# Decode attention: three 64 KiB places that hold K and then V, in place of four 32 KiB buffers and a weight buffer

## The chip, the cores and the metric

The kernel runs on one core of a Trainium2 chip. The metric is device time in microseconds (us), one execution at a time, given as the median and the range of several executions.

Engines: PE is the matrix engine (PEld its weight loads), DVE the vector engine, ACT the scalar engine, SP the engine that issues DMA transfers. "Landing" is the arrival of a transfer.

## The reference, cut to what matters

One token, 16 heads, 65536 cached keys a head, 256 numbers a key, all bf16. K and V together are 1.07 GB, and every byte is used once.

```python
# x [1,1,448]; k_cache, v_cache [1,16,65536,256]; wq [448,4096]; wo [4096,448]
# w1 [448,1792]; w2 [1792,448]
xn = layernorm(x)
q  = (xn @ wq).reshape(1, 1, 16, 256).transpose(0, 2, 1, 3)
p  = softmax(einsum("bhqd,bhkd->bhqk", q, k_cache) * 256 ** -0.5)
s  = einsum("bhqk,bhkd->bhqd", p, v_cache)      # then heads joined, @ wo
g  = silu(silu(xn @ w1) @ w2)
return x + s * g
```

## The kernel before

The keys of a head are cut into four blocks of 128 x 128 keys, so there are 64 blocks. Of each block a partition holds 128 keys. K and V come in half blocks: a row of 64 keys x 256 x 2 bytes is 32 KiB a partition, 4 MiB in all. Four such buffers, two for K and two for V, hold them, and a fifth, W, holds weights.

DVE works through a half block in two steps of 32 keys. In each step it multiplies the last 13 keys with the query in one wide product, which ACT then sums key by key, and does the other 19 as fused dot products. PE weighs V with the softmax weights. Each block keeps its own maximum; the blocks of a head are joined at the end.

```python
KT, SUB, ND, TPB = 64, 32, 19, 2
Kt = [pool.tile([P, KT * Dh], bf16, name=f"K{t}") for t in range(TPB)]
Vt = [pool.tile([P, KT * Dh], bf16, name=f"V{t}") for t in range(TPB)]
W = pool.tile([P, max(DF * HD + HD // 2, NHA * D, KT * Dh)], bf16, name="W")
prod = [pool.tile([P, NA, Dh], bf16, name=f"prod{i}") for i in range(2)]
# ... (small tiles cut)

def sp_block(i):
    for t in range(TPB):
        take(sp, kf[t])                       # K buffer free?
        sp.dma_start(out=Kt[t][:, :], in_=src(Kd, i, t)).then_inc(kl[t], 16)
        take(sp, vf[t])
        sp.dma_start(out=Vt[t][:, :], in_=src(Vd, i - 1, t)).then_inc(vl[t], 16)

def dve_block(i, first=False, halves=False):
    # ... (query copy, waits cut)
    for t in range(TPB):
        for s in range(2):
            m = dve.tensor_tensor(out=prod[k % 2][:, :, :], ...)   # 13 keys, for ACT
            m.then_inc(mr, 1)
            for j in range(ND):                                    # 19 keys
                ins = dve.tensor_tensor_reduce(out=junk_d[jk][:, :], ...)
    # ... copy of the scores, maximum

with nc.Fori(1, NBLK - 1, 1, engines={ET.PE, ET.DVE, ET.Activation, ET.SP}, ...) as i:
    sp_block(i)
    dve_block(i)
    act_block(i)
    # ... PE: maximum, V of the block before, turn of the output
```

## Time and profile before

| | before |
|---|---|
| time, median of 4 (range) | 2529.26 us (2528.97 to 2529.54) |
| span of the profiled execution | 2527.2 us |
| HBM read | 1084.29 MB |
| DMA, mean over the span | 429 GB/s |
| K or V transfers of 4 MiB | 251 |
| packets of 32 KiB / median duration of one | 32128 / 1218 ns |
| last input landed | 2519.7 us |

The prediction below shows the main views: a DMA row of nines, so the time is reading. Two more lines of the page of the kernel before, the busy times and the packet count, will be set against those of the kernel after:

```profile
PE 1284.5 (51%) x4945; PEld 483.4 (19%) x4945; DVE 2219.2 (88%) x10276; ACT 1446.6 (57%) x6996; POOL 1.4 (0%) x12
...
DMA packets 40450, 1084.46 MB, mean 429 GB/s; under 512 B 4338, under 2 KB 6516, under 8 KB 6644
```

The first gives, for each engine, busy microseconds, share of the span and number of instructions. DVE at 88% is the engine nearest to becoming a bound; everything else has room.

### The profile page before, as it was taken

What the parts mean: (1) busy time and instruction counts of PE and PEld (TensorE: products, weight loads), DVE (VectorE), ACT (ScalarE), POOL (GpSimd) and SP (SyncE); (2) the same over time, 40 slices, a digit from 0 to 9 for tenths busy, and PEclk for the clock granted to TensorE, in tenths of its full rate; (3) what the DMA queues carried; (4) which work ended last, traced back from release to release, by engine and by line L of the source; (5) the groups of instructions that cost most, each with busy time, mean ns of one, the idle gap of its engine ahead of it and who ended that gap; (6) DMA issues with size and microseconds to landing.
All of it is one profiled execution on the core that took longest, in us unless ns stands there. A gap on an engine that the chain in (4) does not pass through costs nothing. (4 is left out here: it accounts for less than half of the span.)

```text
span 2527.2 us, 30558 instructions
## 1 busy us (share of the span) xinstructions
PE 1284.5 (51%) x4945; PEld 483.4 (19%) x4945; DVE 2219.2 (88%) x10276; ACT 1446.6 (57%) x6996; POOL 1.4 (0%) x12
## 2 busy tenths in 40 slices
PE   3554455455544554555455445544554455445547
PEld 1111121111111211111112111111121111111212
DVE  7989898898898988988989889889898898898886
ACT  5656565655565656555656565556565655565553
POOL 0000000000000000000000000000000000000000
PEclk7777777777777777777767776777677767776778
DMA  9999999999999999999999999999999999999998
GB/s 413 432 432 432 432 432 432 432 432 432 432 432 433 432 433 432 432 432 432 432 432 432 432 432 432 432 432 432 432 432 432 432 432 433 432 432 432 432 432 346
DMA packets 40450, 1084.46 MB, mean 429 GB/s; under 512 B 4338, under 2 KB 6516, under 8 KB 6644
## 3 DMA queue, kind: packets, MB, share of 16 engines
q1 hardware_dynamic: 40434, 1084.31, 99.8%
q8 instruction: 4, 0.07, 0.0%
q14 instruction: 10, 0.08, 0.0%
q10 hardware_dynamic: 2, 0.00, 0.0%
HBM read 1084.29 MB, written 0.00 MB: 429 GB/s over the span
## 5 line engine op out<-in xcount | busy, mean ns | idle before, releaser
L262 ACT ACTIVATE junk_a<-prod 128x256 bf16<-128x256 bf16 x3328 | 1330.7, 401 | 746.9 <-ACTq L141 746.9
L308 PE MATMUL psO<-V,PV 128*2 128x512 bf16 x4064 | 1165.2, 458 | 1097.6 <-PEq L141 1097.6
L226 DVE CUSTOM_DVE_ANT_0 junk_d<-K,qcur 128x256 bf16<-128x256 bf16 x4864 | 1698.7, 414 | 0.0
L308 PEld LDWEIGHTS psO<-V,PV 128*2 128x2 bf16 x4064 | 388.4, 97 | 1847.6 <-issue 1520.3
L212 DVE TENSOR_TENSOR prod<-K,qcur 128x3328 bf16<-128x3328 bf16 x256 | 482.9, 1886 | 247.0 <-DVEq L141 247.0
L262 ACT ACTIVATION_READ_ACCUMULATOR junk_a<-prod 128x1 f32 x3328 | 620.0, 186 | 0.0
L226 DVE DVE_READ_ACCUMULATOR2_ANT S<- 128x1 f32 x4864 | 374.2, 77 | 0.0
L295 ACT COPY O<-psO 2x512 f32<-2x512 f32 x64 | 36.8, 574 | 202.4 <-ACTq L141 202.4
L343 PE MATMUL ps_t<-eye,O 2*128 2x1 f32 x520 | 69.6, 251 | 48.4 <-PEq L141 48.4
L343 PEld LDWEIGHTS ps_t<-eye,O 2*128 2x128 f32 x520 | 65.9, 192 | 69.0 <-issue 68.9
L297 ACT COPY hist<-ps_t 128x2 f32 (+1 forms) x65 | 10.4, 160 | 94.9 <-ACTq L141 94.9
L301 PE MATMUL ps_nb<-gmax,ones_row 1*128 1x1 bf16 x65 | 10.3, 159 | 56.1 <-PEq L141 55.6
L191 DVE COPY qcur<-qb 128x256 bf16 (+1 forms) x64 | 14.5, 227 | 25.4 <-issue 15.8
L284 ACT ACTIVATE PV<-S,hist 128x128 bf16<-128x128 f32 (+1 forms) x65 | 26.0, 400 | 2.1
L199 DVE COPY S<-S 128x128 f32<-128x128 f32 (+1 forms) x65 | 14.7, 226 | 9.5
L200 DVE TENSOR_REDUCE rmax<-S 128x1 bf16<-128x128 f32 (+1 forms) x65 | 18.2, 280 | 0.2 <-issue 0.2
L180 DVE TENSOR_REDUCE gmax<-ps_m 1x1 bf16<-1x128 f32 x65 | 17.8, 274 | 0.5 <-DVEq L141 0.5
L301 PEld LDWEIGHTS ps_nb<-gmax,ones_row 1*128 1x128 bf16 x65 | 6.0, 92 | 60.8 <-issue 60.5
L333 PE MATMUL ps_m<-ident,rmax 128*1 128x128 bf16 x65 | 14.3, 220 | 5.7 <-PEq L141 5.7
L488 PE MATMUL ps_a<-xnT,V 128*64 128x1 bf16 x112 | 6.7, 256 | 18.2 <-DMA V<-in_B_w_dram 18.2
L284 ACT ACTIVATION_READ_ACCUMULATOR PV<-S,hist (+1 forms) x65 | 12.1, 186 | 0.0
L488 PEld LDWEIGHTS ps_a<-xnT,V 128*64 128x64 bf16 x112 | 6.6, 210 | 18.7 <-DMA V<-in_B_w_dram 18.7
(65 smaller groups left out, 79.3 us busy)
## 6 DMA issues: line engine op xcount, KB each, us to landing
K<-in_A_k_cache_dram SPq DMA_DIRECT2D x126, 4096.0 KB, 21.3
V<-in_A_v_cache_dram SPq DMA_DIRECT2D x125, 4096.0 KB, 28.7
K<-in_A_k_cache_dram SPq DMA_DIRECT2D x4, 2048.0 KB, 18.5
V<-in_A_v_cache_dram SPq DMA_DIRECT2D x4, 2048.0 KB, 22.9
W<-in_A_v_cache_dram SPq DMA_DIRECT2D x2, 2048.0 KB, 27.3
W<-in_A_wq_dram SPq DMA_DIRECT2D x1, 3072.0 KB, 10.4
K<-in_A_wo_dram SPq DMA_DIRECT2D x3, 896.0 KB, 31.4
V<-in_B_w_dram SPq DMA_DIRECT2D x1, 1568.0 KB, 35.5
```

Source lines behind the costliest of these rows:

```text
L180: dve.reduce_max(out=gmax[0:1, :], in_=ps_m[0:1, :], axis=AX.X).then_inc(gm, 1)
L191: q_t = own(dve.tensor_copy(out=qcur[:, :], in_=qb[:, sub(q0, Dh)]))
L199: dve.tensor_copy(out=S2[:, c0:c1], in_=S[:, c0:c1]).then_inc(f, 1)
L200: dve.reduce_max(out=rmax[:, :], in_=S[:, c0:c1], axis=AX.X).then_inc(rm, 1)
L212: m = dve.tensor_tensor(out=prod[k % 2][:, :, :], in0=Kv[:, s * SUB + ND : (s + 1) * SUB, :], in1=qcur[:, None, :].to_broadcast([P, NA, Dh ...
L226: ins = dve.tensor_tensor_reduce(out=junk_d[jk][:, :], in0=Kv[:, s * SUB + j, :], in1=qcur[:, :], scale=1.0, scalar=0.0, op0=ALU.mult, op1 ...
L262: ins = act.activation(out=junk_a[jk][:, :], in_=prod[k % 2][:, j, :], func=ACT.Identity, accum_out=S[:, a : a + 1],)
L284: act.activation(out=PV[:, c0:c1], in_=S2[:, c0:c1], func=ACT.Exp, bias=neg, scale=scale, accum_out=hist[:, at(i), 1:2].rearrange("p o s - ...
L295: act.copy(out=O[:, :], in_=po[:, :]).then_inc(oc, 1)
L301: pe.matmul(ps_nb[:, 0:1], lhsT=ones_row[0:1, :], rhs=gmax[0:1, :], start=True, stop=True).then_inc(bm, 1)
L308: ins = pe.matmul(po[:, :], lhsT=PV[:, c0 + c : c0 + c + 2], rhs=T[:, (k0 + c) * Dh : (k0 + c + 2) * Dh], start=(start and c == 0), stop=( ...
L343: ins = pe.matmul(ps_t[:, a : a + 1], lhsT=Ov[:, j, a, :], rhs=eye2[:, j : j + 1], start=(j == 0), stop=(j == 1),)
```

## The change

The intent is to move the same bytes in half as many, twice as long transfers. A block's K takes one 64 KiB row a partition, in one of three places. When DVE and ACT have done with it, V of the same block is loaded into the same place, one block late; when PE has done with V, K of the block three later follows. To make room, the products and the unused outputs are written over K itself, and all weights lie in a place that is not used yet (at the start) or no longer (at the end). DVE, ACT, PE and SP each get a loop of their own, three blocks long, because there are three places. At the start w1 comes before wq, and the first K comes in two halves. The diff, cut to its core:

```diff
-KT = 64
+KB = 128
 SUB = 32
 ND = 19
-TPB = 2
+NR = 3
...
-    Kt = [pool.tile([P, KT * Dh], bf16, name=f"K{t}") for t in range(TPB)]
-    Vt = [pool.tile([P, KT * Dh], bf16, name=f"V{t}") for t in range(TPB)]
-    W = pool.tile([P, max(DF * HD + HD // 2, NHA * D, KT * Dh)], bf16, name="W")
-    prod = [pool.tile([P, NA, Dh], bf16, name=f"prod{i}") for i in range(2)]
+    KW, HK = KB * Dh, KB // 2
+    R = [pool.tile([P, KW], bf16, name=f"R{t}") for t in range(NR)]
...
+    def load_k(i, s):
+        take(sp, vf[s])
+        sp.dma_start(out=R[s][:, :], in_=block(Kd, i)).then_inc(kl[s], 16)
+        sp.sem_inc(kh[s], 16)
+
+    def load_v(i, s):
+        take(sp, kf[s])
+        sp.dma_start(out=R[s][:, :], in_=block(Vd, i)).then_inc(vl[s], 16)
...
+            m = dve.tensor_tensor(out=pair, in0=pair, ...)       # in place
...
+                ins = dve.tensor_tensor_reduce(out=Kv[:, c, :], in0=Kv[:, c, :], ...)
...
+        load_rows(w1_t, B_w1, F, dl["w1"])
+        load_rows(wq_t, A_wq, HD, dl["wq"])
+        load_keys(R[0], block(Kd, 0), 0, HK, kl[0])
+        # ... w2
+        load_keys(R[0], block(Kd, 0), HK, KB, kh[0])
+        load_k(1, 1)
+        load_k(2, 2)
+        load_v(0, 0)
+        load_v(1, 1)
+        with loop(ET.SP, NR, LAST - 2, NR) as i:
+            for s in range(NR):
+                load_k(i + s, s)
+                load_v(i + s - 1, (s - 1) % NR)
...
+        with loop(ET.DVE, 0, LAST - 2, NR, hint_back_edge=True) as i:
+            for s in range(NR):
+                dve_block(s)
...
+        with loop(ET.PE, 1, LAST - 4, NR, hint_back_edge=True) as i:
+            for s in range(NR):
+                pe_block(i + s, s)
```

The last block is peeled off the loops, with V in pieces (the last 128 keys as 32, 32, 32, 16, 8, 8) and the projection `wo` behind it.

## The prediction

> **What bounds the kernel now.** I read the page first, then the waits of the DMA-issuing queue, then one iteration in the timeline, then the chain that ended last. The page, top and DMA rows:
>
> ```profile
> span 2527.2 us, 30558 instructions
> ...
> DMA  9999999999999999999999999999999999999998
> GB/s 413 432 432 432 432 432 432 432 432 432 432 432 433 432 433 432 432 432 432 432 432 432 432 432 432 432 432 432 432 432 432 432 432 433 432 432 432 432 432 346
> ...
> HBM read 1084.29 MB, written 0.00 MB: 429 GB/s over the span
> ```
>
> All 16 DMA engines are busy from the first slice to the last but one, at 432 GB/s. 1084.29 MB / 432 GB/s is 2510 us of the 2527. The kernel is bound by its reads; only some 17 us are not the steady stream. The issues show that each transfer is queued well ahead:
>
> ```profile
> K<-in_A_k_cache_dram SPq DMA_DIRECT2D x126, 4096.0 KB, 21.3
> V<-in_A_v_cache_dram SPq DMA_DIRECT2D x125, 4096.0 KB, 28.7
> ...
> SPq L141 <- SPq L141: 2316.3, 251, 24.3
> ```
>
> 4 MiB moves in 4.19 MB / 432 GB/s = 9.7 us, yet takes 21 to 29 us from issue to landing, so 12 to 19 us of that is queue ahead of it. The last line, from the waits of the issuing queue, says that SP itself waits nearly all the time for a buffer to come free; that costs nothing while the queue is so deep. This depth is what the change spends. Next the work that frees buffers:
>
> ```profile
> L262 ACT ACTIVATE junk_a<-prod 128x256 bf16<-128x256 bf16 x3328 | 1330.7, 401 | 746.9 <-ACTq L141 746.9
> L308 PE MATMUL psO<-V,PV 128*2 128x512 bf16 x4064 | 1165.2, 458 | 1097.6 <-PEq L141 1097.6
> L226 DVE CUSTOM_DVE_ANT_0 junk_d<-K,qcur 128x256 bf16<-128x256 bf16 x4864 | 1698.7, 414 | 0.0
> ```
>
> and one buffer (half a block) in the timeline near 1000 us:
>
> ```profile
> 1003.84 1.89 DVE L212 TENSOR_TENSOR prod<-K,qcur 128x3328 bf16<-128x3328 bf16 x1 [2.52 <-DVEq L141]
> 1012.22 1.89 DVE L212 TENSOR_TENSOR prod<-K,qcur 128x3328 bf16<-128x3328 bf16 x1
> 1013.45 9.00 PE L308 MATMUL psO<-V,PV 128*2 128x512 bf16 x32 [10.95 <-PEq L141]
> 1020.82 0.23 DVE L199 COPY S<-S 128x128 f32<-128x128 f32 x1
> 1021.29 0.33 SPq L174 DMA_DIRECT2D K<-in_A_k_cache_dram  x1
> ```
>
> The reader is to see: one DVE step (one product, 19 dot products) is 1012.22 - 1003.84 = 8.38 us; from the start of DVE on a landed buffer to the issue that reuses it is 1021.29 - 1003.84 = 17.45 us for two steps, hence 17.45 + 2 x 8.38 = 34.2 us for four. The K landing before it had its last of 16 engines done at 1003.13 in the packet records, 0.7 us ahead of DVE. Last, the end, from the timeline:
>
> ```profile
> 2512.39 3.62 PE L308 MATMUL ps_a<-W,PV 128*2 128x512 bf16 x16
> 2515.84 1.68 PE L679 MATMUL ps_ao<-K,OT 128*1 128x448 bf16 x8
> 2518.48 4.70 PE L679 MATMUL ps_ao<-K,OT 128*1 128x448 bf16 x24
> ...
> 2523.22 0.61 DVE L688 TENSOR_TENSOR tmp<-ps_ao,g_f 1x448 f32<-1x448 f32 x1 [3.71 <-PE ps_ao L679]
> 2523.86 0.61 DVE L692 TENSOR_TENSOR out_bf<-tmp,x_f 1x448 bf16<-1x448 f32 x1
> 2524.50 0.33 SPq L696 DMA_DIRECT2D out_dram<-out_bf  x1
> ```
>
> In the packet records the first data packet starts at 2.0 us and the last input lands at 2516.0 us. So 11.2 us of the span come after the data: PE is behind by then.
>
> [...]Here the first issue starts at 0.96 and the first packet at 2.0 us, so I use 1.1. [...]in the burst at 1013.45 the first ten weight loads are 0.43 us apart, later ones 0.21. [...]The trace has such packets, of 8 and 16 KB, but none between 83 and 2467 us[...]. Each one seen stretches the data packet behind it: the two at 57.4 and 82.7 us cost one and the same DMA engine 333 ns plus 657 ns each.
>
> **The change, part by part.**
> *Buffers.* K of a block (8 MiB, 8.39 / 0.432 = 19.4 us) goes into a place; when DVE is done, its V goes into the same place; when PE is done, the K of three blocks later. Order in the queue: K(i+1), V(i), K(i+2), V(i+1). A pair takes 38.8 us. V(i) may start when K(i+1) is in, 19.4 + 19.4 = 38.8 us after K(i) landed. It is ready to start 0.7 (wake) + 34.2 (DVE) + 1.1 (first packet) = 36.0 us after. Slack 2.8 us. K(i+2) may start 58.2 us after K(i) landed. Before it: DVE done at 34.7, maximum through PE and back 1.3 (0.95 us from rmax to broadcast in the old tail, plus rmax), then V(i-1) on PE: 64 matmuls, ten at 0.43 and 54 at 0.216, 16.0 us, then 0.3 + 1.1 to the first packet: 53.4. Slack 4.8 us. So the queue goes from 12 to 19 us of lead to 2 to 3, but does not run dry: 0 us per block.
> *In-place results and no ring of small junk tiles.* Same durations expected: DVE 1.89 us and 0.346 us a dot product, ACT 5.2 us per 13, below DVE's 8.4. 0 us.
> *Start.* The same bytes in another order. K0 lands later, DVE begins near 26.6 instead of 18.1 us. The tightest point is V1: DVE ends block 1 near 96.7, first packet at 97.8, wanted 97.5. Plus 0.5 us.
> *Packets.* 32 KiB packets last 1218 ns, 16 KiB ones 613, so 8 ns of each are fixed. Rows of 64 KiB, if they go as one packet, save at most 2008/2 x 8 = 8 us per engine; packets overlap by some 5 ns and they may be split. I take -2.
> *Tail.* Counting from the landing T of K 61 (blocks 0 to 63): the last data lands at 77.6 (K 63) + 38.8 (V 62, V 63) + 10 (wo, small rows) = 126.4. DVE ends 63 at 114.7, with 4.4 us of head weights between the halves; softmax near 117, keys 64 to 95 land 118.5 and take 3.5, turn 1.1, last 16 matmuls 3.5, copy and four heads, turn 1.1, two heads and DVE 1.4: 131.5; output 2.7: 134.2. Tail 7.8 instead of 11.2: -3.4.
> Sum: -3.4 + 0.5 - 2 = -5. 2529.3 - 5 = 2524 us.
>
> **The rivals.** *A. Instruction fetch.* DVE's loop grows from some 172 instructions[...] to 3 x 166 plus a few, about 503[...]. If two pieces are read anew per iteration, 2 x 0.99 x 21 = 42 us more on one DMA engine, and every transfer waits for its slowest engine: 2566 us. If all five, 104 us: 2628.
> *B. DVE or PE becomes the bound.* If the lead is too small because a step lasts longer than I took it (slower in-place writes, ACT late because it now waits for PE's output in mid-block), each us beyond the 2.8 delays the pair by at least half: 2 us over is 1 us x 62, 2586 us. For it: slack of only 7% of a pair. Against: every term is measured, and ACT has 3 us to spare per step.
> *C. Nothing but the tail.* Packets are split, the stream is the same: 2526.
>
> **Range and chances.** [...]over 2% faster is all but excluded: 0.01. My own theory or C, 2512 to 2530, gets about 0.7; A in its small form 0.12, in its large one 0.08; B 0.1, half of it under 2%. Slower by 2% is over 2580: 0.12. Same 0.87. The range of 8 in 10 goes from 2512 to 2566.
>
> **What would show each step right or wrong.** Right: DMA row of nines and 432 GB/s throughout; K to landing about 22 us and V about 22 (19.4 plus a lead of 2 to 3); DVE steps of 8.4 us; last data near 2515 us and 8 us after it. A: instruction-fetch packets in every iteration, one DMA engine lagging more and more, GB/s lower everywhere. B: gaps in the DMA row at regular intervals, with SP issuing right after DVE or PE and the first packet after the queue ran empty. I am wrong if the stream's rate moves by over 1% in either direction.

-3.4 + 0.5 - 2 is -4.9, put as -5, hence 2524. The readings from the trace that the terms use: 1.1 us from the first issue to the first packet (0.96 to 2.0 us), matmuls 0.43 us apart at first and 0.216 later. "Such packets" are packets of the instruction queues. A "piece" in rival A is one of them of 8 KB, and its 0.99 us are the 333 ns of the packet and the 657 ns by which the data packet behind it is longer (1875 ns for 1218). How many pieces might be read anew in an iteration was a guess of mine, and that over 2% was excluded was an estimate: no trace had shown either.

## The result

| | before | after |
|---|---|---|
| median of 4 (range) | 2529.26 us (2528.97 to 2529.54) | 2526.19 us (2525.35 to 2527.04) |
| ratio, 95% interval | | 0.9988 (0.9971 to 1.0005): same |
| span of the profiled execution | 2527.2 us | 2523.2 us |
| last input landed | 2519.7 us | 2515.4 us |
| from there to the end of the span | 7.5 us | 7.8 us |

Ratios in this document, with their intervals, are those from the fast runs of the same rounds; they are not quite the ratios of the medians quoted. Here and below "landed" comes from the single DMA packets recorded in the trace; the semaphore that a waiting engine sees follows some 0.4 us later (for the last piece of V in the kernel after 2515.86 us, against 2515.41).

The page of the kernel after, its top and DMA rows:

```profile
span 2523.2 us, 29918 instructions
...
PE 1198.1 (47%) x5125; PEld 500.5 (20%) x5125; DVE 2233.7 (89%) x10281; ACT 1443.9 (57%) x6992; POOL 2.5 (0%) x13
...
DMA  9999999999999999999999999999999999999998
GB/s 423 417 430 433 434 431 433 433 432 432 432 432 432 433 434 437 434 435 433 433 433 432 432 432 432 432 433 434 439 434 433 433 433 433 432 432 432 432 412 346
DMA packets 22728, 1084.52 MB, mean 430 GB/s; under 512 B 2354, under 2 KB 4532, under 8 KB 4916
```

The row of nines is unchanged and the middle slices lie about 1 GB/s higher on average (single ones scatter from 430 to 439), but the second slice (417) and the last but one (412) now show dents, losses of rate, that were not there. The packet count fell by 17,700: the 64 KiB rows go as single packets, 15872 of them with a median of 2420 ns.

The lead, how long before its turn a transfer is issued, is what the change spent. From the DMA view of the kernel after (count, median us from issue to landing):

```profile
R<-in_A_k_cache_dram SPq DMA_DIRECT2D x62, 25.5
R<-in_A_v_cache_dram SPq DMA_DIRECT2D x62, 23.8
```

An 8 MiB transfer itself takes 19.35 us (from landing to landing), so K is issued 6.1 us and V 4.4 us before its turn, where before it was 12 to 19 us. That figure counts to the slowest of the 16 DMA engines; it is looked at more closely with experiment F. SP still only waits for places to come free: 2395.9 us in 126 waits.

```profile
SPq L154 <- SPq L154: 2395.9, 126, 35.1
```

The work itself did not change its pace. Groups by line (count, busy us, mean ns of one, idle before), then one block in the timeline:

```profile
L249 DVE CUSTOM_DVE_ANT_0 R<-R,qcur 128x256 bf16<-128x256 bf16 x4864 | 1700.2, 417 | 0.0
L271 ACT ACTIVATE R<-R 128x256 bf16<-128x256 bf16 x3328 | 1330.7, 401 | 697.1 <-ACTq L154 697.1
```

```profile
999.71 1.89 DVE L238 TENSOR_TENSOR R<-R,qcur 128x3328 bf16<-128x3328 bf16 x1
1008.09 1.88 DVE L238 TENSOR_TENSOR R<-R,qcur 128x3328 bf16<-128x3328 bf16 x1
1016.46 1.88 DVE L238 TENSOR_TENSOR R<-R,qcur 128x3328 bf16<-128x3328 bf16 x1
...
1025.06 0.23 DVE L224 COPY S<-S 128x128 f32<-128x128 f32 x1
...
1025.43 0.33 SPq L197 DMA_DIRECT2D R<-in_A_v_cache_dram  x1
```

A DVE step is still 8.38 us (1008.09 - 999.71), and SP's issue of the V that reuses the place starts 0.37 us after DVE's copy did. Writing over K shows no cost: 417 ns a dot product where it was 414, and the same step.

The end, from the chain that ended last in the kernel after (start, us, what):

```profile
2484.34 23.09 DMA R<-in_A_v_cache_dram
2507.43 0.04 issue
2507.47 3.61 PE bank L318 x16
2511.08 1.03 PE bank L346 x8
2512.11 3.54 PE bank L318 x16
2515.66 1.51 PE bank L662 x8
2517.17 1.03 PE bank L346 x8
2518.20 0.95 PE bank L662 x4
2519.18 0.62 DVE R L744
2519.82 0.61 DVE x_f L746
```

A landing of V sets it off, and PE's chain runs from there to the end.

### Where the microseconds went

From the packet records I took the landing of given amounts of data on the slowest DMA engine, and compared it with a line of 433.4 GB/s, chosen near the 433 GB/s of the loop, from the first packet at 2.0 us. The excess over that line, in us:

| after so many MB have landed | before | after | gained in this stretch |
|---|---|---|---|
| 57.2 (start) | 4.29 | 5.27 | -1.0 |
| 971.6 (loop) | 12.87 | 4.92 | +8.9 |
| 1063.9 (in the kernel after: last K in) | 13.64 | 8.74 | -3.0 |
| 1084.3 (all) | 15.90 | 11.59 | -0.6 |

So the loop gained 8.9 us (12.87 - 4.29 became 4.92 - 5.27), and 4.6 of them were given back in three other places; the data landed 4.3 us earlier. The tail after it is 0.3 us longer. That makes the 4.0 us by which the profiled spans differ; the medians differ by 3.1.

The two dents can be seen. Three stretches of the kernel after (us, then busy us of PE, PEld, DVE, ACT, POOL, then granted PE clock, DMA share, GB/s):

```profile
60.00:100.00 40.00, 3.33 (x14) 2.34 (x14) 38.43 (x171) 23.12 (x112) 0.00 (x0) 0.50 0.98 414
1000.00:1500.00 500.00, 231.96 (x970) 96.31 (x969) 448.13 (x2063) 290.20 (x1409) 0.00 (x0) 0.70 1.00 433
2440.00:2480.00 40.00, 28.43 (x131) 11.95 (x129) 32.10 (x145) 21.40 (x103) 0.00 (x0) 0.83 0.92 388
```

The packet records place the first gap at 96.1 to 98.9 us: SP issued V of block 1 at 96.8, when the queue was running out, and its first packet started at 97.7. The second is at 2441.1 to 2444.3 us, with no DMA engine at work for part of it. It begins with PE. From PE's timeline:

```profile
2420.18 1.44 PE L318 MATMUL bank<-R,PV 128*2 128x512 bf16 x3
2427.17 15.35 PE L318 MATMUL bank<-R,PV 128*2 128x512 bf16 x61 [5.55 <-issue]
2442.35 0.17 PE L368 MATMUL bank<-ident 128*1 128x1 bf16 x1
```

and from SP's:

```profile
2442.65 0.82 SPq L201 DMA_DIRECT2D R<-in_A_k_cache_dram  x2
```

PE stands still for 5.55 us after three of the 64 matmuls of a block, waiting for nothing that the trace shows; a 16 KiB packet of the instruction queue starts at 2424.64 and takes 1.07 us. PE has left its loop by then (the last branch of the loop is at 2394.41) and is in the code behind it. The place is therefore free 5.5 us late, and the last K is issued into a queue already empty. DVE has a stall of the same size at its own exit (last branch at 2458.66), with an 8 KiB instruction packet at 2463.76:

```profile
2458.56 0.28 DVE L214 TENSOR_REDUCE gmax<-bank 1x1 bf16<-1x128 f32 x1 [0.94 <-DVEq L154]
2465.61 0.42 DVE L231 CAST qcur<-bank 128x256 bf16<-128x256 f32 x1 [6.77 <-DVEq L154]
```

### The profile page after: what moved, and what is told of

The parts are those of the page before. It is cut to its first block, busy times and chain, and to the rows that moved or that the text cites. A ratio compares the mean times of both kernels' runs of the same rounds, so it can differ in the third digit from the quotient of the medians.

```text
span 2523.2 us, 29918 instructions
## 1 busy us (share of the span) xinstructions
PE 1198.1 (47%) x5125; PEld 500.5 (20%) x5125; DVE 2233.7 (89%) x10281; ACT 1443.9 (57%) x6992; POOL 2.5 (0%) x13
## 5 line engine op out<-in xcount | busy, mean ns | idle before, releaser
L271 ACT ACTIVATE R<-R 128x256 bf16<-128x256 bf16 x3328 | 1330.7, 401 | 697.1 <-ACTq L154 697.1
L249 DVE CUSTOM_DVE_ANT_0 R<-R,qcur 128x256 bf16<-128x256 bf16 x4864 | 1700.2, 417 | 0.0
L318 PE MATMUL bank<-R,PV 128*2 128x512 bf16 x4096 | 1023.7, 416 | 32.4 <-DMA R<-in_A_v_cache_dram 15.3
L238 DVE TENSOR_TENSOR R<-R,qcur 128x3328 bf16<-128x3328 bf16 x256 | 482.6, 1885 | 198.7 <-DVEq L154 198.6
L271 ACT ACTIVATION_READ_ACCUMULATOR R<-R 128x1 f32 x3328 | 620.2, 186 | 2.6 <-issue 2.6
L330 PE MATMUL bank<-ident,rmax 128*1 128x128 bf16 x65 | 17.1, 263 | 1021.6 <-PEq L154 1021.6
L318 PEld LDWEIGHTS bank<-R,PV 128*2 128x2 bf16 x4096 | 365.0, 90 | 663.1 <-issue 208.0
L346 PE MATMUL bank<-eye,O 2*128 2x1 f32 x536 | 98.0, 300 | 236.8 <-PEq L154 236.8
L330 PEld LDWEIGHTS bank<-ident,rmax 128*1 128x1 bf16 x65 | 5.2, 79 | 1026.1 <-issue 1025.9
L346 PEld LDWEIGHTS bank<-eye,O 2*128 2x128 f32 x536 | 94.2, 257 | 254.8 <-issue 254.8
L231 DVE CAST qcur<-bank 128x256 bf16<-128x256 f32 x64 | 27.2, 425 | 20.2 <-DVEq L154 18.3
L297 ACT COPY O<-bank 2x512 f32<-2x512 f32 x67 | 37.5, 559 | 9.1 <-ACTq L154 9.1
```

What stands on the lines that cost most here:

```text
L231: dve.tensor_copy(out=qcur[:, :], in_=ps_q).then_inc(sd, 1)
L238: m = dve.tensor_tensor(out=pair, in0=pair, in1=qcur[:, None, :].to_broadcast([P, NA, Dh]), op=ALU.mult,)
L249: ins = dve.tensor_tensor_reduce(out=Kv[:, c, :], in0=Kv[:, c, :], in1=qcur[:, :], scale=1.0, scalar=0.0, op0=ALU.mult, op1=ALU.add, accum ...
L271: ins = act.activation(out=prod, in_=prod, func=ACT.Identity, accum_out=S[:, c : c + 1],)
L297: act.copy(out=O[:, :], in_=po).then_inc(oc, 1)
L318: ins = pe.matmul(po, lhsT=PV[t][:, c : c + 2], rhs=R[s][:, c * Dh : (c + 2) * Dh], start=(start and c == k0), stop=(stop and c == k1 - 2),)
```

## The experiments

Twelve kernels ran, and all gave the correct result. Three sets shared a chip and the runs of the kernel before: A to D; E with `delay2`, `nohint_all` and `nd20`; G with `delay1` and `nd14_short`. Each is compared with the kernel before of its own rounds; where two experiments of different sets are compared with each other or with the kernel after, this rests on the medians of the kernel before being the same within 0.2 us.

### A. The kernel after once more

No edit: how well does the result repeat?

> The changed kernel unaltered, to be compared with its variants on the same chip. 2525 to 2527 us, in the profile a DMA gap of about 2.2 us near 2440 us (16-engine mean) and one of about 1.1 us near 97 us.

Measured: 2527.89 us (2526.31 to 2531.17), the kernel before 2529.41; ratio 0.9997 (0.9983 to 1.001). It is 1.7 us slower than in the first comparison, and its executions differ among themselves by nearly 5 us, where nine of the kernel before spread over 3. A gain of 3 us is thus at the edge of what these runs resolve, and the account by stages above says more than the ratio. The profile repeats the dents: 1.48 us lost at 95 to 100 us, 0.47 at 115, 2.84 at 2440.

### B. The stall at PE's loop exit

The back-edge hint (`hint_back_edge=True`) is one more instruction an iteration in the trace of the kernel after (21 on DVE, 21 on ACT, 20 on PE), which stands at the head of the loop. Here PE's loop loses it:

```diff
-        with loop(ET.PE, 1, LAST - 4, NR, hint_back_edge=True) as i:
+        with loop(ET.PE, 1, LAST - 4, NR) as i:
```

> The changed kernel with the back-edge hint taken from PE's loop alone. Theory (the 5.5 us stall of PE at 2421.6 us is a fetch of the code behind the loop[...] and it is what empties the DMA queue at 2440 us): stall and gap go, about 2 to 3.5 us less than the changed kernel, some 2523. Rival[...]: stall stays, same time.[...]

Measured: 2527.22 us (2524.63 to 2530.2), ratio 0.9991 (0.9977 to 1.0005). PE's stall is gone:

```profile
2421.59 15.37 PE L318 MATMUL bank<-R,PV 128*2 128x512 bf16 x64
```

All 64 matmuls run in one piece, the DMA gap at 2440 is gone, there are no instruction packets in the loop after 143 us (so PE's loop, now of 477 instructions, brings none without the hint), and the last input lands at 2513.5 us, 3.4 earlier than in A's profile (2516.9). The time did not follow. The chain that ended last in this kernel no longer contains a transfer:

```profile
2505.60 0.22 PE bank L330
2505.82 1.57 PE bank L662 x6
2507.39 0.11 PE bank L336
2507.50 1.58 PE bank L662 x4
2509.08 0.52 PE bank L649 x2
2509.60 3.66 PE bank L318 x16
```

L330 is the maximum of DVE's last half block, which DVE had finished only at 2505.1 us: PE waits for DVE, whose own exit stall (6.2 us here) is still there, and the data waits for PE. The tail after the last landing is now 11.9 us (2525.4 - 2513.5). So PE's stall and the DMA gap come with the hint on PE's loop (5.55 us of stall with it, none without), which is shown; removing it alone gains nothing that can be measured, since DVE sets the end next.

### C. The gap at the start

The first half of K of block 0 in two quarters, so that DVE can begin earlier:

```diff
-        load_keys(R[0], block(Kd, 0), 0, HK, kl[0])
+        load_keys(R[0], block(Kd, 0), 0, SUB, kl[0])
+        load_keys(R[0], block(Kd, 0), SUB, HK, kq[0])
...
+            if k == 1:
+                take(dve, kq[s], 16)
```

> The changed kernel with the first half of the first K cut in two, so that DVE begins a quarter block earlier (near 22 instead of 27 us). Theory (the gap near 97 us is DVE ending block 1 some 2 us too late for V of block 1): DVE ends it near 92 us, the gap goes, about 1 us less than the changed kernel. Rival (the DMA engine that lags because of instruction fetches at the start sets the pace anyway): same time within 0.5 us.

Measured: 2526.22 us (2524.66 to 2526.86), ratio 0.9986 (0.9972 to 0.9999). The gap at 97 us is gone, but one of 1.39 us appears at 115 to 120, where K of block 3 waits for its place. The start is held back by a chain of places, not by one event, and mending the first link moves the gap to the next.

### D. Both together

The edits of B and C.

> Both of the above together. If both gaps cost what the 16-engine means say, 3 us or a little more less than the changed kernel, near 2523 us, and 6 us less than the kernel before.

Measured: 2525.42 us (2524.48 to 2529.55), ratio 0.9988 (0.9975 to 1.0002), span of the profile 2522.4. The four kernels of these rounds cannot be told apart: their medians lie within 2.5 us and their ranges overlap.

### E. Is it the length of the packets?

Everything as in the kernel after, but each K and V transfer issued as two, of half rows (32 KiB):

```diff
-        sp.dma_start(out=R[s][:, :], in_=block(Kd, i)).then_inc(kl[s], 16)
-        sp.sem_inc(kh[s], 16)
+        load_keys(R[s], block(Kd, i), 0, HK, kl[s])
+        load_keys(R[s], block(Kd, i), HK, KB, kh[s])
...
-        sp.dma_start(out=R[s][:, :], in_=block(Vd, i)).then_inc(vl[s], 16)
+        load_keys(R[s], block(Vd, i), 0, HK, vl[s])
+        load_keys(R[s], block(Vd, i), HK, KB, vl[s])
...
-        take(pe, vl[s], 16)
+        take(pe, vl[s], 32)
```

> The changed kernel with every K and V block read by two transfers of half a row each, so packets of 32 KiB again, all else the same. Theory (the stream is faster because a 64 KiB packet takes 2420 ns and two of 32 KiB 2 x 1213 to 1218): a block transfer takes 19.43 instead of 19.35 us, 126 of them 8 to 10 us more, near 2535 us, slower than the kernel before. Rival (the rate changed because of the order of transfers or fewer semaphore writes): 19.35 us stays, no more than 2 us change.

Measured: 2534.47 us (2533.85 to 2537.56), the kernel before 2529.28; ratio 1.0025 (1.0009 to 1.0042).

```profile
span 2532.7 us, 30180 instructions
...
DMA packets 40584, 1084.53 MB, mean 428 GB/s; under 512 B 4338, under 2 KB 6516, under 8 KB 6900
```

The packet count is that of the kernel before again, and three blocks take 116.55 us in the loop, against 116.11 with whole rows. That is 0.147 us a block, 9.1 us over 62 blocks. The gain of the loop is therefore the long rows and not the places or the loops. (Twice as many transfers come with half as long packets, and this run does not part the two. The packets' own times fit: 2420 ns against 2 x 1216 in this run, 8 a transfer and DMA engine, so 0.1 us, of which 0.073 shows.) It also tells what the rest of the change costs: with the old packets, the new structure is 5 us slower than the kernel before.

### F. How much slack do the places leave?

An idle DVE instruction (a maximum over data that nobody uses) after the first product of each block, 1.08 us in `delay1` and 2.15 us in `delay2`. Both are below the 2.8 us of slack that the prediction counted.

```diff
             m.then_inc(mr, 1)
+            if k == 0:
+                dve.reduce_max(out=idle, in_=ident[:, None, :].to_broadcast([P, 15, P]), axis=AX.XY)
```

(`delay1` has 7 in place of 15.) The larger one first:

> The changed kernel with one extra reduction on DVE per block (15 x 128 elements, near 2 us), whose result nobody reads. Theory (2.8 us of slack on the way K landed - DVE - V issued, counted for the DMA engine that lags): no change beyond 2 us. Rival (the slack that counts is that of the engine in front, 1.7 us, or DMA efficiency falls when the queue gets short): several tenths of a us per block, 10 to 40 us more.

Measured: 2598.02 us (2592.69 to 2603.75), ratio 1.0267 (1.0247 to 1.0287), slower. My expectation missed by 70 us. Then the smaller:

> The changed kernel with one extra reduction of 7 x 128 elements on DVE per block, near 1.05 us. The 2.15 us of the longer one cost 70 us though I had counted 2.8 us of slack. New theory: the slack that counts is that of the DMA engines in front, 1.7 us in the changed kernel's trace (issue at 1025.43 plus 1.0, K landed on the first engine at 1028.2), and once they run dry all engines restart together with slow packets of about 3.2 instead of 2.4 us. Then 1.05 us still fits: no more than 5 us. Rival (any delay of DVE costs in proportion): 34 us.

Measured: 2559.27 us (2557.98 to 2560.91), the kernel before 2529.29; ratio 1.012 (1.0104 to 1.0135). Again my theory missed, and the rival, a cost in proportion, hit: 32 us over the 2527 of the kernel after (a value between its two medians, used from here on). The added row, and the stretch of the loop, of `delay1`:

```profile
L249 DVE TENSOR_REDUCE idle<-ident 128x1 bf16<-128x896 bf16 x64 | 69.2, 1082 | 0.0
```

```profile
1000.00:1500.00 500.00, 238.70 (x988) 98.07 (x988) 455.11 (x2051) 286.62 (x1391) 0.00 (x0) 0.70 1.00 428
```

The DMA engines are at a share of 1.00 and yet move 428 GB/s in place of 433: they are mostly slow rather than idle. In the packet records, packets after a late issue last 2.5 to 4.3 us instead of 2.42, and the mean of the loop's packets is 2446 ns against 2422, which is 1.0 of the 1.4% lost; the rest is idle time. So the row of nines hides this loss, and so would a search for gaps.

For each V transfer in the loop I then took how long before the end of the transfer ahead of it SP had issued it, counted to the DMA engine that finished first and to the one that finished last (medians, us):

| kernel | lead, first engine | lead, last engine | us a transfer |
|---|---|---|---|
| nd17 (G below) | 4.54 | 5.28 | 19.35 |
| after | 2.81 | 3.99 | 19.35 |
| nd14_short (H below) | 1.88 | 3.65 | 19.60 |
| delay1 | 1.60 | 3.53 | 19.62 |
| delay2 | 0.93 | 3.12 | 19.95 |

With 2.8 us nothing is lost, with 4.5 nothing is gained, and with 1.9 and less each transfer takes 0.25 to 0.6 us longer. The lead that is needed lies between 1.9 and 2.8 us on the first engine (by the last engine, between 3.65 and 3.99; the delays move both, so these runs do not tell which one counts). The single transfers of `delay1` and `nd14_short` narrow it down: the 25 V transfers with over 2.0 us of lead on the first engine lost 0.01 us on average, the 72 with 1.0 to 2.0 lost 0.57. So the kernel after has at most 0.9 us of the slack that I had put at 2.8. The cost is (2559.27 - 2527) / 62 = 0.52 us a block for 1.08 of delay, and (2598.02 - 2527) / 62 = 1.15 for 2.15: about half of the whole delay, as if there were no slack. The half can be worked out from the order of the queue, though no run shows it apart: from the landing of K(i) to that of K(i+2), two blocks on, the chain holds one pass of DVE and two transfers, V(i) and K(i+2), so a pass that is longer by some time makes two blocks longer by it.

### G. Fewer dot products on DVE: more lead, and a shorter loop

`ND`, the dot products of a step on DVE, from 19 to 17; ACT gets 15 of 32 keys. A step of DVE becomes shorter, and its loop goes from 501 to 453 instructions.

```diff
-ND = 19
+ND = 17
```

> The changed kernel with 17 dot products a step on DVE and 15 on ACT. DVE's step shrinks from 8.38 us by 2 x 0.346 and grows by 2 x 0.14: near 7.97, so a block ends near 1.5 us earlier; loop 453 instructions[...]. Theory (DVE's end of block is what leaves the DMA queue short at 97 us, and DVE's last two blocks are on the path that sets the end): the gap near 97 us goes, DVE ends its last block near 3 us earlier, 1 to 3 us less than the changed kernel. Rival (the end hangs on the last V pieces landing): less than 1 us.

Measured: 2523.05 us (2521.93 to 2524.05), the kernel before 2529.29; ratio 0.9974 (0.996 to 0.9988). The lead grew to 4.54 us, the gap at 97 us is gone (one of 1.86 us at 115 to 120 took its place), DVE's exit stall is gone as well although the hint is still there, and the last input lands at 2513.6 us, 1.8 earlier than in the kernel after, with the same 7.8 us behind it. PE still stands still for 4.45 us at its exit, but the dent at 2440 us falls from 2.2 to 0.5 us: there the longer lead covers the stall. Then the same with the edit of B:

> 17 and 15, and the hint taken from PE's loop. If both DMA gaps are gone and DVE is early enough for the last V pieces, the data end near 2511 us of the span and the rest is PE behind them: 3 to 5 us less than the changed kernel, near 2522 us. If PE alone sets the end, no better than the one above.

Measured: 2522.61 us (2522.36 to 2523.19), ratio 0.9974 (0.996 to 0.9987); last input at 2512.6 us. **This version beats both kernels**: by 6.7 us that before (the interval excludes 1), and by 3.6 us the median of the kernel after, whose fastest execution of nine, 2525.35, is slower than the slowest of these five. It was not timed in the same rounds as the kernel after, only beside the same kernel before. Whether B's edit adds to `ND = 17` is not settled: 0.4 us lies within the ranges. Nor is it settled how much of the gain is the lead and how much DVE's exit, for the edit changes both; in the loop itself the longer lead gains nothing (19.35 us a transfer in both).

### H. What do instruction packets in the loops cost, and when do they come?

The rival A of the prediction was that the longer loops fetch their instructions anew. The kernel after shows no instruction packet between 109 and 2424 us. Two ways to make it happen: take the hint from every loop, or make DVE's loop longer with `ND = 20` (525 instructions an iteration in place of 501).

```diff
-        with loop(ET.DVE, 0, LAST - 2, NR, hint_back_edge=True) as i:
+        with loop(ET.DVE, 0, LAST - 2, NR) as i:
...        # likewise ACT and PE
```

> The changed kernel without the hint on all three compute loops. [...]8 KB instruction packets in each of 21 iterations, 42 us more (two per iteration) to 104 us more (five), or a stall of DVE at each back edge. [...]same time, less the 2 to 3 us of PE's stall at loop exit.

(Two outcomes: packets or stalls with 42 to 104 us more, or the same time less the stall at PE's exit.)

Measured: 2626.44 us (2626.0 to 2628.56), ratio 1.0388 (1.0371 to 1.0406).

> The changed kernel with 20 instead of 19 dot products a step on DVE and 12 instead of 13 on ACT. DVE's work per block grows by 4 x (0.346 - 1.89/13) = 0.8 us, inside the slack of about 2.8, so by the work alone the time stays. But DVE's loop grows by 24 to 525 instructions[...]: 8 KB instruction packets in every iteration, two to five on one DMA engine at 0.7 to 1 us each, 30 to 100 us more. If not: same time within 2 us.

Measured: 2628.31 us (2625.97 to 2628.65), ratio 1.0391 (1.0373 to 1.0408). Both are 100 us slower than the kernel after. The queue that carries instructions, first in the kernel after, then in these two (packets, MB, share), and of the two the wait of DVE where its loop begins again (us, times, longest):

```profile
q14 instruction: 14, 0.11, 0.0%
```

```profile
q14 instruction: 114, 0.93, 0.1%
...
DVE qcur L231 <- DVEq L154: 132.3, 21, 7.1
```

```profile
q14 instruction: 115, 0.94, 0.1%
...
DVE qcur L231 <- DVEq L154: 17.7, 21, 5.8
```

A hundred packets of 8 KB more, about five in each of some twenty iterations. Without the hint DVE stands still for 6.3 us (132.3 / 21) at each return; with 525 instructions and the hint it does not (17.7 us in all, as in the kernel after), and the time is the same. What the two share is that the DMA engines drift apart: the spread between the first and the last to finish a transfer is 4.5 us without hints and 3.7 with `ND = 20`, against 1.2 in the kernel after (medians of the leads as in F), and the V lead on the first engine falls to 0.6 us. This fits the rival as written: one DMA engine carries the instruction packets (the two of 8 KB at 57.4 and 82.7 us in the kernel before lie on one engine, by the handoffs of its packets) and each transfer waits for it. A spread alone need not cost anything: the kernel before, with its long lead, has one of 3.6 us and the same pace as `split_rows` (116.60 and 116.55 us for three blocks). No run parts the lag from the short lead on the first engine, but the two traces go some way. The engine that finishes last never had less than 4.9 us (no hints) and 4.0 us (`nd20`) of lead for a V transfer, no less than the 3.9 of the kernel after, so it did not wait for SP; and yet it took 20.2 us a transfer. An estimate from the prediction's reading of an instruction packet (0.99 us) gives 5 x 0.99 / 6 = 0.83 us for each of the six transfers of an iteration, and 20.2 - 19.35 is 0.85. Against it, `nd20` also lengthens DVE's step from 8.38 to 8.59 us, and 4 x 0.21 = 0.84 us a block, by half and 62 times as in F, would be 26 us of its 100.

A last kernel asks whether a short loop needs the hint: `ND = 14` (380 instructions), no hint on PE and DVE.

> 14 dot products on DVE and 18 on ACT, hint taken from the loops of PE and DVE. DVE's loop then has 380 instructions[...]: no instruction packets in the loop in spite of the missing hint, and DVE's stall of about 6 us at its loop exit (idle before the cast at 2465.6 us in the changed kernel, with an 8 KB instruction packet at 2463.8) goes. Rival[...]: packets and about 100 us more, as without hints. ACT, with 7.1 us a step, ends the block near where DVE ended it, so the loop keeps its pace; the end 2 to 4 us earlier, near 2523 us.

Measured: 2560.15 us (2555.37 to 2565.32), ratio 1.0128 (1.0113 to 1.0144). The expectation of 2523 was missed, for a reason that I should have counted. DVE in the loop:

```profile
1001.95 0.23 DVE L224 COPY S<-S 128x128 f32<-128x128 f32 x1 [4.66 <-DVEq L154]
```

At the end of each block DVE waits some 5 us for ACT, which now sums 18 keys a step; the place comes free late and the lead is 1.88 us (table in F). The question itself was answered: no instruction packets in the loop (after 147 us) although no hint is given, and no stall of DVE at the exit. Without the hint, then, DVE's loop of 380 instructions brought no packets and that of 501 (`nohint_all`) about five an iteration. (The missing stall is not the hint's doing alone: with the hint kept and 453 instructions, in G, it was missing too.)

## Why the prediction was right, and which steps of it were not

The time (2524.0 predicted, 2526.19 measured), its class and its range were right. The sum of -5 us was near the 3 to 4 measured (1.5 in the rounds of A), but three of its terms were off, one was left out, and they cancelled: that the number came out was luck.

- **What bounds the kernel.** Right: 432 GB/s before, 433 after, DMA at nine tenths in all but the last slice.
- **Buffers, 0 us a block.** The value was right. The arithmetic of the lead was right too: taking its own first-packet time back out, it gives V a lead of 2.8 + 1.1 = 3.9 us on the slowest engine and K 4.8 + 1.1 = 5.9; measured were 3.99 and 5.76. The step that failed is "Slack 2.8 us". It took 1.1 us as the time from issue to the first packet, from the first transfer of the program, with no other under way. What has to be covered in the loop is 1.9 to 2.8 us on the first engine (F). The slack was all but used up, and the claim stood by luck.
- **In-place results, 0 us.** Right: 1.89 us a product as before, 417 ns a dot product against 414, a step of 8.38 us.
- **Start, +0.5.** The place and the hour were right (V of block 1, DVE done at 96.7 us as predicted, the copy being at 96.47). The size was +1.0 by the ledger; most packets right after the gap lasted 2.7 to 3.3 us and not 2.42, which I had not counted.
- **Packets, -2.** The mechanism was right and the size was not. The rows were not split, and packets of 64 KiB take 2420 ns, 16 less than two of 32 KiB in the kernel before (not the 8 ns taken from the step from 16 to 32 KiB). A transfer of 8 MiB takes 19.352 us in place of 2 x 9.717 = 19.434, so 126 x 0.082 = 10 us; the ledger shows 8.9 in the loop, and E puts it at 9.1.
- **Tail, -3.4.** Failed. "The last input lands at 2516.0 us" was a misreading of the packet records, in which I had left out the last group of completions; it is 2519.7. The tail before was 7.5 us, not 11.2. The 7.8 predicted for after was exact, so the term is +0.3.
- **Left out.** The exits of the hinted loops. PE's stall of 5.55 us left the queue dry, 3.0 us in the ledger. B shows that DVE's exit stood right behind it, so that taking PE's away alone earns nothing that can be measured.
- **Rival A** did not happen, but its large form, 2628 us for five instruction packets an iteration, is what both ways of provoking it gave (2626.4 and 2628.3).
- **Rival B** did not happen either. Its rule, half of each us beyond the slack, fits both delays of F; its threshold was nearer to 0 than to 2.8.
- **Rival C** gave 2526 for the wrong reasons: the packets were not split, and nothing came from the tail.

## What to carry to other kernels

Longer contiguous rows gained 0.4% here, in a kernel bound by its reads (DMA row of nines, 432 GB/s), and the buffers that hold them cost lead; count the lead against what a transfer needs under load (here between 1.9 and 2.8 us on the first engine), and measure it by adding a known delay before trusting it. A share of DMA time of 1.00 does not show that nothing is lost: compare GB/s (428 in `delay1` against 433, both at 1.00). When a loop is unrolled, count its instructions on each engine, look for instruction packets in the loop and for stalls at its exit, and leave some room. Here PE stood still for 4.45 to 5.55 us after leaving its hinted loop, DVE for 6.2 to 6.8 us with 501 instructions and not at all with 453, and a hundred instruction packets in the loop came with 100 us more; two dot products a step moved to another engine gave as much as the whole change.
